# Stage 0 turned before it is decayed, four more diagonals on GpSimd, and a new order for the prologue of an RWKV-5 + MLP kernel

## The chip, the cores and the metric

The kernel runs on one core of a Trainium2 chip. A core has five engines with their own instruction streams: TensorE (PE; its weight loads are shown as PEld), VectorE (DVE), ScalarE (ACT), GpSimd (POOL) and SyncE (SP). They wait for one another by semaphores. DMAs are issued by SP, ACT and POOL. The metric is the device time of one execution in microseconds (us); lower is better. Times are medians of several executions; the profile is of one.

## The reference

Two operators, one after the other. The first is a linear attention with a decaying state, over B = 4 batches, H = 8 heads, S = 768 tokens, D = 48 channels:

```python
for t in range(S):
    kt, vt, rt = (k[:, :, t].copy(), v[:, :, t].copy(), r[:, :, t].copy())
    cur = np.einsum('bhd,bhe->bhde', u[None] * kt, vt)
    y[:, :, t] = np.einsum('bhd,bhde->bhe', rt, state + cur)
    state = w[None, :, :, None] * state + np.einsum('bhd,bhe->bhde', kt, vt)
```

The second takes y as 3072 rows of 384 and computes `h = x @ w_in` (384 to 2048), `g = maximum(0.01 * h, h)` and `g @ w_out` (2048 to 384).

## The kernel before

**Stages.** The recurrence is done in chunks of L = 128 tokens. A stage n is one chunk of one batch (chunk n // 4, batch n % 4), 24 stages in all. Within a chunk, r is multiplied by powers of w rising with the token (`qtab`) and k by falling powers (`ktab`), both centred on token 64, so that one matrix product gives the decayed scores. The letters of the list ORDER stand for these steps of a stage:

- k, r, v: loads, by DMA from POOL's queue with a cast to bf16 (stage 0's k and r come in fp32 from ACT's and SP's queues into `k_f`, `r_f`);
- P (`prep_half`, q for r and k for k): DVE multiplies by the table into the tile `qk`;
- T and t (`turn_mm`, `turn_out`): TensorE turns four pairs of heads into a PSUM bank, ACT (or DVE, with an @) copies it to `tp`; X..T (`turn_dma`) does both by a DMA transpose from SP's queue, from stage TURNED = 8 on;
- A and M (`a_mm`, `a_mask_half`): the scores, in two PSUM banks, and their masking into `at`, half a for the even heads and half b for the odd;
- the diagonal (the term with u), in two ways. For n < DIAG: X, D, Q (`diag`, `diag_mm`, `scaled_v`): DVE multiplies the turned halves, four small matmuls sum over channels, DVE scales v into `vs`, and three extra matmuls (L550) add it in `y_mm`. From DIAG on: q and Q (`row_sums`, `diag_tile`): DVE makes the token sums in three steps (L373, L375, L377), POOL writes them as diagonal matrices into both halves of `at` (L384), and M lays the masked scores over them with `copy_predicated` (L436), so that M waits for POOL too;
- Y and y (`y_mm`, `y_out`): the chunk's output, turned, in PSUM, and its copy to `xT` by ACT; K and S (`kv_mm`, `state`): the new state;
- G, J, H (`g1`, `g1_pair`, `g2`) and g, j, h: the MLP for one stage by quarters, for a pair of stages by eighths (J), and the second product; ACT does the evictions (`Prelu`), SP's queue the output DMA. F n is n fill matmuls on `ones`, whose results nobody reads.

**What sets the order.** There is no scheduler. The prologue is the list ORDER: each token adds its instructions to the streams of their engines, in that order, and `Sched` derives the semaphore waits from what is read and written. An engine does its instructions strictly in order, so an instruction that waits holds up all that stand behind it on its engine: on POOL that is compute and the issue of loads alike. PSUM has eight banks of 2 KB in a free list: `take` pops the next one when a token is listed and `give` appends it, so which mask or eviction frees the bank of a later matmul group is fixed by the list. The pair loop after it (L696 to L722) handles stages 2m and 2m + 1 in turn m, from m = FIRST // 2 = 3: eight J groups, the diagonals of the two stages `ahead` (2m + 4, 2m + 5), loads for `far` (2m + 8), P and the transposes for `later` (2m + 6), then H, A, Y, M, K, S and H. At m = 3 stages 10 and 11 are ahead, 12 and 13 later, 14 and 15 far; the list ends with the masks of 9 and 8 and the loads of 12 and 13. The first groups of J take the banks that are free, and the fifth to the eighth those that the four masks of stages 9 and 8 give back, in the order in which these are listed.

**Constants.** w is loaded as one row (`w_row`) and spread over the partitions by two fp32 matmuls of 192 columns (L295), whose logarithm times the token number gives the tables by exponentials on ACT. A copy by heads (`w_head`, `w8`), and its product with u, are turned by small matmuls (`columns_mm`) into columns for the state's decay (`wl`) and the diagonal (`wu`). The identity and the triangle are made by POOL from `ones`.

## Time and profile before

| | us |
|---|---|
| median of 3 executions (lowest, highest) | 170.09 (169.96, 170.54) |
| the profiled execution | 170.54 |
| its span in the profile | 168.8 |
| TensorE busy | 164.0 (97%) |
| DVE / ACT / POOL busy | 107.6 / 92.5 / 103.8 |
| first L619 of the pair loop (m = 3) starts | 53.52 |
| last matmul ends | 166.5 |

The busy table gives each engine's time at work, and the slices show it in tenths of 40 equal parts of the span (4.2 us each). The chain that ended last follows back from the last instruction to what released it; here it is nearly all TensorE. A timeline row gives start, length, engine, line, operation, tiles and count of instructions; in a merged row the length is that of the group. L384 is POOL's diagonal product, L222 its loads, L375 and L373 DVE's row-sum products. The profile does not show which PSUM bank a matmul takes; that follows from the list.

### The profile page before, as it was taken

The page shows a single profiled execution, that of the slowest core. Times are in us where ns is not written, and L with a number is a line of the kernel's source. Part 1 is how long each engine was busy: PE and PEld are TensorE (multiplying, and loading weights), DVE is VectorE, ACT ScalarE, POOL GpSimd, SP SyncE. Part 2 cuts the span into 40 slices and gives each one's busy share as a digit, 9 for nine tenths or more (in the row PEclk, how much of TensorE's full clock was granted, in tenths as well). Part 3 has the DMA queues.
Part 4 walks back from the last instruction along what each step waited for, and adds up shares of the span by engine and source line. Part 5 has one row for each costly group of instructions (what it writes and reads, how often), then busy time and mean ns, then how long its engine had stood idle before and what let it go on. Part 6 is the DMA issues. An engine that isn't in the chain of part 4 may idle for free.

```text
span 168.8 us, 4933 instructions
## 1 busy us (share of the span) xinstructions
PE 164.0 (97%) x2127; PEld 124.4 (74%) x2127; DVE 107.6 (64%) x215; ACT 92.5 (55%) x172; POOL 103.8 (61%) x117
## 2 busy tenths in 40 slices
PE   5999999899999999999999999999999999999994
PEld 3577899798667867867867867768768668668663
DVE  7379989884376999999859959969866050000000
ACT  3855899587123933933834835735637538449221
POOL 7999999990059979897993993993707200000000
PEclk9999999999999999999999999999999999999999
DMA  6999999999999999969999299299941011011022
GB/s 106 155 170 133 163 163 173 185 190 149 110 177 144 161 62 153 193 82 169 126 140 171 55 143 177 65 109 131 147 122 50 0 50 47 0 50 47 25 74 93
DMA packets 99146, 19.67 MB, mean 117 GB/s; under 512 B 92338, under 2 KB 99124, under 8 KB 99124
## 3 DMA queue, kind: packets, MB, share of 16 engines
q0 software_dynamic: 76512, 10.03, 93.1%
q1 hardware_dynamic: 21554, 9.12, 25.2%
q8 instruction: 17, 0.28, 0.6%
q10 hardware_dynamic: 1058, 0.20, 0.6%
q14 instruction: 5, 0.04, 0.1%
HBM read 20.45 MB, written 4.72 MB: 149 GB/s over the span
## 4 chain that ended last, share of the span: by engine, by line
PE 96%; DVE 1%; issue 1%; ACT 0%; DVEq 0%
PE ps L643 37%; PE ps L619 31%; PE ps L596 6%; PE ps L557 6%; PE ps L423 4%; PE ps L260 2%; PE ps L464 2%; PE ps L398 2%; PE ps L295 1%; PE ps L550 1%; DVE v_sb L280 1%; PE ps L451 1%; PE ps L321 0%; DVE qk L344 0%; ACT out_sb L655 0%
## 5 line engine op out<-in xcount | busy, mean ns | idle before, releaser
L643 PE MATMUL ps<-w_out_sb,gT 128*128 128x384 bf16 (+2 forms) x400 | 65.7, 320 | 0.0
L619 PE MATMUL ps<-xT,w_in_sb 128*128 128x256 bf16 x480 | 54.3, 273 | 0.0
L643 PEld LDWEIGHTS ps<-w_out_sb,gT 128*128 128x128 bf16 x400 | 37.9, 98 | 22.1
L619 PEld LDWEIGHTS ps<-xT,w_in_sb 128*128 128x128 bf16 x480 | 46.7, 98 | 6.5 <-ACT xT L571 0.2
L384 POOL TENSOR_TENSOR at<-ident,s_tok 128x512 bf16<-128x512 bf16 x32 | 35.0, 1121 | 26.8 <-DVE s_tok L377 26.8
L629 ACT ACTIVATE gT<-ps 128x512 bf16<-128x512 f32 x80 | 47.8, 597 | 6.2 <-PE ps L619 1.3
L655 ACT ACTIVATE out_sb<-ps 128x384 f32<-128x384 f32 (+2 forms) x25 | 11.9, 477 | 52.9 <-PE ps L643 52.9
L436 DVE CAST_PREDICATED at<-mask,ps 128x512 bf16<-128x512 uint16 x32 | 19.9, 684 | 15.5 <-PE ps L423 15.5
L222 POOL DMA_DIRECT2D v_sb<-in_v_dram x24 | 22.5, 953 | 0.0
L222 POOL DMA_DIRECT2D k_sb<-in_k_dram x23 | 21.6, 947 | 0.0
L222 POOL DMA_DIRECT2D r_sb<-in_r_dram x23 | 21.1, 943 | 0.0
L571 ACT ACTIVATE xT<-ps 128x384 bf16<-128x384 f32 x24 | 11.0, 492 | 6.5 <-PE ps L557 6.5
L344 DVE TENSOR_TENSOR qk<-r_sb,qtab 128x384 bf16<-128x384 bf16 x23 | 13.4, 592 | 1.9 <-DMA r_sb<-in_r_dram 1.9
L344 DVE TENSOR_TENSOR qk<-k_sb,ktab 128x384 bf16<-128x384 bf16 x23 | 13.9, 606 | 0.0
L375 DVE TENSOR_TENSOR rku<-r_sb,ku 128x384 bf16<-128x384 bf16 x16 | 12.7, 794 | 0.5
L525 DVE TENSOR_TENSOR sum_t<-ps,st 128x384 bf16<-128x384 f32 x16 | 8.8, 550 | 5.2 <-PE ps L464 5.2
L596 PE MATMUL ps<-xT,w_in_sb 128*128 128x128 bf16 x192 | 12.0, 219 | 0.0
L557 PE MATMUL ps<-at,v_sb 128*32 128x128 bf16 x384 | 11.1, 219 | 0.6 <-issue 0.6
L432 DVE TENSOR_TENSOR at<-ps,mask 128x512 bf16<-128x512 f32 x16 | 10.5, 682 | 0.9 <-PE ps L423 0.9
L606 ACT ACTIVATE gT<-ps 128x512 bf16<-128x512 f32 x16 | 9.6, 600 | 2.7 <-PE ps L596 2.1
L596 PEld LDWEIGHTS ps<-xT,w_in_sb 128*128 128x128 bf16 x192 | 10.9, 98 | 0.1
L557 PEld LDWEIGHTS ps<-at,v_sb 128*32 128x32 bf16 x384 | 8.7, 97 | 1.1 <-issue 0.7
(60 smaller groups left out, 131.7 us busy)
## 6 DMA issues: line engine op xcount, KB each, us to landing
out_dram<-out_sb SPq DMA_DIRECT2D x23, 192.0 KB, 3.9
v_sb<-in_v_dram POOLq DMA_DIRECT2D x24, 96.0 KB, 6.0
r_sb<-in_r_dram POOLq DMA_DIRECT2D x23, 96.0 KB, 5.6
k_sb<-in_k_dram POOLq DMA_DIRECT2D x23, 96.0 KB, 5.1
w_in_sb<-in_moe_w_in_dram POOLq DMA_DIRECT2D x4, 384.0 KB, 5.6
w_out_sb<-in_moe_w_out_dram POOLq DMA_DIRECT2D x4, 384.0 KB, 7.9
tp<-qk SPq DMA_TRANSPOSE x16, 4.6
k_f<-in_k_dram ACTq DMA_DIRECT2D x1, 192.0 KB, 2.8
```

Of the source, the lines that this page charges most:

```text
L222: add("pool", lambda: G.dma_start(dst, src), R=pace, W=[(which, n)], dma=f"{which}{n}")
L344: add("dve", lambda: V.tensor_tensor(qk[iq][:, H * half:H * half + H, 0:D], hd(src), hd(tab[:, :]), ALU.mult), R=[(name, n), ("qk"[half] + ...
L375: add("dve", lambda: V.tensor_tensor(rku[i2][:, :], r_of(n), ku[i2][:, :], ALU.mult), R=[("r", n), ("ku", i2)], W=[("rku", i2)])
L384: add("pool", lambda hh=hh, s_of=s_of: G.tensor_tensor(at[ia][:, hh, :, :], ident[:, :].unsqueeze(1).to_broadcast([128, NP, 128]), s_of.un ...
L436: add("dve", lambda: V.copy_predicated(at[n % NAT][:, hh, :, :], mask[:, :].bitcast(mybir.dt.uint16).unsqueeze(1).to_broadcast([128, NP, 1 ...
L557: last = PE.matmul(ps_y[32 * q:32 * q + 32, 128 * s:128 * s + 128], a, m, start=not whole and step == 0, stop=step == len(columns[q]) - 1)
L571: add("act", lambda: A.activation(xT[m % NX][:, :, 128 * half:128 * half + 128], ps_y[:, 0:HD].rearrange("p (s t) -> p s t", t=128), AF.Copy),
L596: last = PE.matmul(ps_g[:, 128 * f:128 * f + 128], w_in_sb[:, s, 128 * fb:128 * fb + 128], xT[ix][:, s, t], start=s == 0, stop=s == NSL - 1)
L619: last = PE.matmul(ps_g[:, 256 * f:256 * f + 256], w_in_sb[:, s, 128 * fb:128 * fb + 128], xT[ix][:, s, :], start=s == 0, stop=s == NSL - 1)
L629: add("act", lambda: A.activation(gT[ig][:, 2 * j:2 * j + 2, :].rearrange("p f t -> p (f t)"), ps_g[:, :], AF.Prelu, alpha=0.01), R=[key], ...
L643: last = PE.matmul(ps_o[:, 0:c1 - c0], gT[ig][:, s, 128 * half:128 * half + 128], w_out_sb[:, s, c0:c1], start=s == 0, stop=s == NFB - 1)
L655: add("act", lambda: A.activation(out_sb[io][:, c0:c1], ps_o[:, 0:c1 - c0], AF.Copy), R=[key], W=held)
```

## The change

Stage 0 (n < RAW = 1): r and k are cast to bf16 without any table (`cast`, into the new tile `raw`: k by ACT, token c0k, and r by DVE, c0q@), turned by TensorE, and decayed when they leave PSUM: DVE multiplies the bank by the new table `turned`, which holds the powers of w with channels on the partitions and tokens along the row. ACT makes it by four exponentials of the token rows `trow`, each scaled by one column of log w (token E). P of r is no longer done for stage 0; P of k is, later, for the state.

DIAG goes from 8 to 4: stages 4 to 7 get their diagonals by `row_sums` and `diag_tile`, without D, `prod`, `vs` and L550.

The constants are made differently: `w_head` is loaded twice side by side and turned in one step per half of the partitions (Cw, and Cu for its product with u); the row of w is loaded as halves in partitions 0 and 64, spread by one matmul each into adjacent banks, and has one logarithm and one exponential per table; the identity, its 8x8 corner and the triangle come from comparisons on DVE of `trow` with `tcol`; the u loads move from ACT's to SP's queue, and the order of the loads on SP is w8, r0, w, u8, u. `ones` and the fill matmuls have 128 columns instead of 256. The prologue's order is listed anew, loads included; the pair loop's code is the same.

```diff
 FIRST, NB, PACE = 6, B, 3
-TURNED, DIAG, CARRY, EXACT = 8, 8, 4, 1
+TURNED, DIAG, CARRY, EXACT, RAW, VISIT, LATE = 8, 4, 4, 1, 1, 3, 3
 ORDER = """
-w k0 r0 u8 w8 u ones tcol wi0 v0z r2 table exps one id wlz qk0 F6 bcA r1 id8 F2 bcB lnA k1 u16 wu8 ktabA F1 Cm k2 lnB U
-qtabA ktabB v0 utab P0k qtabB Wl wi3 F6 T0k P0q W C tri t0k@ F1 T0q v1 P1q t0q P2q F6 T1q X0 r3 A0 P1k t1q T2q M0a T1k
-k3 t2q D0 P2k F1 K0 t1k Q0 T2k v2 M0b t2k F1 A1 X1 v5 F2 Y0 X2 M1b A2 k4 y0 D2 M1a D1 K1 G0.0 k5 Q1 M2b G0.3 g0.0 wi1
-P3q Y1 P3k g0.3 r4 S1 T3q y1 K2 Q2 T3k t3q v3 G1.3 S2 t3k M2a G1.0 r5 g1.3 P4k Y2 X3 g1.0 r8 P5k A3 S0 y2 K5 M3b r6 T5k
-G2.3 t5k S5 k7 G2.0 g2.3 M3a G1.1 k9 g2.0 P4q G0.1 g1.1 wi2 T4k g0.1 D3 P5q K3 r7 T4q Q3 t4k T5q G2.1 S3 t5q k6 P8q Y3
-t4q P6q X5 A5 v4 g2.1 P7k A4 X4 y3 D5 T6q M4a wo3 T7k t6q G3.0 M5a v8 t7k G3.3 Q5 g3.0 wo0 M5b D4 G3.1 g3.3 P9k k8 G2.2
-M4b g3.1 P7q G1.2 wo2 g2.2 P6k T7q v6 g1.2 T6k t7q@ K4 Y5 t6k Q4 wo1 A7 y5 X6 A6 k11 S4 Y4 M7b v9 D6 y4 G3.2 M6a v10
-J2.4 M6b g3.2 J2.3 M7a v11 j2.4 J2.5 X7 j2.3 r10 D7 J2.1 j2.5 q8 r9 J2.2 j2.1 J2.6 r11 j2.2 P8k J2.0 j2.6 v7 X8T K8 Q6
-K6 j2.0 G0.2 k10 S6 Y6 g0.2 S8 J2.7 y6 H1 j2.7 P11k K9 H2 h1 S9 P10q H0 h2 P9q q9 X9T P11q K7 Q9 H3 Q7 h0 X11T S7 P10k
-X10T Q8 Y7 h3 A9 y7 A8 M9a M8a M9b M8b k12 r12 v12 k13 r13 v13
+w8 k0 r0 w u8 u wlz tcol trow qk0 r3 table tri id8 k1 ones F6 zr Cw exps v0z Wl id r1 W v0y c0k wi1 E one F13 T0k c0q@
+r2 bc wu8 Cu v0 lnw T0q C t0k u16 k3 qtab t0q F3 U ktab k2 P1q F3 A0 utab P3q X0 T1q v2 P0k M0a D0 T3q t1q v1 P1k M0b
+t3q F5 T1k wi3 P2q F2 K0 Q0 t1k wi2 T2q S0 A1 t2q v3 X1 Y0 P3k P2k D1 k5 M1b y0 T3k T2k t3k K2 M1a G0.1 k4 t2k X3 A3 Q1
+g0.1 A2 r4 D3 S2 Y1 M2b r5 K1 y1 G0.3 M2a v5 X2 G1.1 g0.3 S1 v4 D2 G1.3 M3a g1.1 M3b G0.2 wi0 g1.3 Q2 K3 r7 G1.2 g0.2
+Q3 S3 Y2 wo3 g1.2 P5k Y3 P4k y2 v9 T5k P4q y3 G2.1 q4 wo1 t5k G3.2 g2.1 wo0 G3.1 g3.2 k8 P5q T4q q5 g3.1 T4k T5q Q4
+G2.2 t4q t4k G3.3 g2.2 t5q@ G1.0 g3.3 P7q Q5 A4 g1.0 A5 G2.3 M4b G3.0 g2.3 M4a K5 k9 T7q g3.0 M5a G2.0 t7q M5b wo2 K4
+Y4 g2.0 S4 k7 Y5 y4 G0.0 S5 y5 r9 J2.4 g0.0 r8 J2.5 j2.4 J2.6 k6 j2.5 J2.3 j2.6 r6 P8k J2.7 j2.3 P9k v6 J2.2 j2.7 v8 K9
+J2.0 j2.2 S9 J2.1 v7 j2.0 H1 j2.1 q7 r11 r10 v11 P7k P8q P9q T7k X8T h1 H3 P6k Q7 P6q t7k X9T q6 k10 K6 K7 h3 T6q k11
+S6 T6k t6q K8 H2 S8 t6k v10 P11q Q6 S7 P10q A6 h2 A7 H0 M7b M6b P10k M7a X10T M6a Y7 q9 h0 Y6 y7 A8 y6 A9 P11k Q9 q8
+X11T Q8 M9b M9a M8a M8b k12 r12 v12 k13 r13 v13
 """
...
+    def twice(h):
+        return dram(h, 0, [[D, H], [0, 2], [1, D]])
+
     def tokens():
-        add("pool", lambda: G.iota(tcol[:, :], pattern=[[0, 1]], base=0, channel_multiplier=1,
+        add("pool", lambda: G.iota(tcol[:, :], pattern=[[0, 1]], base=-MID, channel_multiplier=1,
                                    allow_small_or_imprecise_dtypes=True), W=["tcol"])
+
+    def token_rows():
+        for half, (sign, base) in enumerate(((1, -MID), (-1, MID - 1))):
+            add("pool", lambda half=half, sign=sign, base=base: G.iota(
+                trow[:, half, :], pattern=[[sign, 128]], base=base, channel_multiplier=0,
+                allow_small_or_imprecise_dtypes=True), W=[("trow", half)])
...
 
         def emit():
             for _ in range(n):
-                last = PE.matmul(ps[i][:, 0:256], ones[:, 0:128], ones[:, 0:256], start=True, stop=True)
+                last = PE.matmul(ps[i][:, 0:128], ones[:, :], ones[:, :], start=True, stop=True)
             return last
 
         add("pe", emit, R=["ones"], W=[("ps", i), f"fill{n}"])
 
     def identity():
-        add("pool", lambda: G.affine_select(ident[:, :], ones[:, 0:128], pattern=[[1, 128]], compare_op=ALU.is_equal,
-                                            fill=0.0, base=0, channel_multiplier=-1), R=["ones"], W=["ident"])
+        add("dve", lambda: V.tensor_scalar(ident[:, :], trow[:, 0, :], tcol[:, 0:1], None, ALU.is_equal),
+            R=["tcol", ("trow", 0)], W=["ident"])
 
     def triangle():
-        add("pool", lambda: G.affine_select(mask[:, :], ones[:, 0:128], pattern=[[1, 128]], compare_op=ALU.is_ge,
-                                            fill=0.0, base=-1, channel_multiplier=-1), R=["ones"], W=["mask"])
+        add("dve", lambda: V.tensor_scalar(mask[:, :], trow[:, 0, :], tcol[:, 0:1], None, ALU.is_gt),
+            R=["tcol", ("trow", 0)], W=["mask"])
+
+    def small_identity():
+        add("dve", lambda: V.tensor_scalar(ident8[:, :], trow[0:H, 0, 0:H], tcol[0:H, 0:1], None, ALU.is_equal),
+            R=["tcol", ("trow", 0)], W=["ident8"])
 
...
-    half_bank = {}
-
-    def spread_w(half):
-        ps_w, key = half_bank[half] = take()
-        cols = slice(192 * half, 192 * half + 192)
-        add("pe", lambda: PE.matmul(ps_w[:, cols], one_row[:, :], w_row[:, cols], start=True, stop=True),
-            R=["one_row", "w_row"], W=[key])
-
...
+    w_bank = []
+
+    def spread_w():
+        for half in range(2):
+            w_bank.append(take())
+        assert w_bank[1][1][1] == w_bank[0][1][1] + 1
+
+        def emit():
+            for half in range(2):
+                at0 = slice(64 * half, 64 * half + 1)
+                last = PE.matmul(w_bank[half][0][:, 0:192], one_row[at0, :], w_row[at0, :], start=True, stop=True)
+            return last
+
+        add("pe", emit, R=["one_row", "w_row"], W=[w_bank[0][1], w_bank[1][1]])
...
+    def table(dst, exps, name, read):
+        add("act", lambda: A.activation(dst[:, :], lnw[:, :], AF.Exp, scale=exps[:, 0:1]),
+            R=["lnw", read], W=[name + "tab"])
+
+    def turned_table():
+        for p in range(NP):
+            add("act", lambda p=p: A.activation(turned[:, p:2 * NP:NP, :], trow[:, :, :], AF.Exp,
+                                                scale=wcol[:, p:p + 1]),
+                R=["wcol", ("trow", 0), ("trow", 1)], W=[("turned", p)])
...
+    def cast(half, eng):
+        dst, src = raw[:, H * half:H * half + H, 0:D], hd((r_of, k_of)[half](0))
+        if eng == "dve":
+            add("dve", lambda: V.tensor_copy(dst, src), R=[("rk"[half], 0)], W=[("raw", half)])
+        else:
+            add("act", lambda: A.activation(dst, src, AF.Copy), R=[("rk"[half], 0)], W=[("raw", half)])
+
     turn_bank = {}
 
     def turn_mm(n, half):
-        iq = n % NQK
+        src, reads = qk[n % NQK], [("kp" if half else "qp", n % NQK), ("qk0", n % NQK)]
+        if n < RAW:
+            src, reads = raw, [("raw", half), "raw0"]
         ps_t, key = turn_bank[n, half] = take()
...
     def turn_out(n, half, eng):
         it = n % NTP
         ps_t, key = turn_bank[n, half]
         dst = tp[it][:, NP * half:NP * half + NP, :].rearrange("p m t -> p (m t)")
-        if eng == "dve":
+        if n < RAW:
+            tab = turned[:, NP * half:NP * half + NP, :].rearrange("p m t -> p (m t)")
+            add("dve", lambda: V.tensor_tensor(dst, ps_t[:, :], tab, ALU.mult),
+                R=[key] + [("turned", p) for p in range(NP)], W=[("tp", it, half)])
+        elif eng == "dve":
             add("dve", lambda: V.tensor_copy(dst, ps_t[:, :]), R=[key], W=[("tp", it, half)])
         else:
             add("act", lambda: A.activation(dst, ps_t[:, :], AF.Copy), R=[key], W=[("tp", it, half)])
...
-    def columns_mm():
-        ps_c, key = c_bank["c"] = take()
+    def w_columns():
+        ps_c, key = c_bank["w"] = take()
 
         def emit():
             for hh in range(2):
-                rows = slice(64 * hh, 64 * hh + D)
-                PE.matmul(ps_c[rows, 0:H], w_head[:, :], ident8[:, :], start=True, stop=True)
-                last = PE.matmul(ps_c[rows, H:2 * H], wu_head[:, :], ident8[:, :], start=True, stop=True)
-            return last
-
-        add("pe", emit, R=["w_head", "wu_head", "ident8"], W=[key])
...
+                last = PE.matmul(ps_c[64 * hh:64 * hh + 64, 0:NP], w_head[:, hh, :], ident8[:, hh:H:2],
+                                 start=True, stop=True)
+            return last
+
+        add("pe", emit, R=["w_head", "w_gap", "ident8"], W=[key])
+
+    def wu_columns():
+        ps_c, key = c_bank["u"] = take()
+
+        def emit():
+            for hh in range(2):
+                last = PE.matmul(ps_c[64 * hh:64 * hh + D, 0:NP], wu_head[:, :], ident8[:, hh:H:2],
+                                 start=True, stop=True)
+            return last
+
+        add("pe", emit, R=["wu_head", "ident8"], W=[key])
...
+        ps_c, key = c_bank["w"]
+        add("act", lambda: A.activation(wcol[:, :], ps_c[:, 0:NP], AF.Ln), R=[key], W=["wcol"])
+        give(key)
...
-        "w": lambda: add("sp", lambda: SP.dma_start(w_row[:, :], row(w)), W=["w_row"], dma="w"),
-        "w8": lambda: add("sp", lambda: SP.dma_start(w_head[:, :], by_head(w)), W=["w_head"], dma="w8"),
-        "u8": lambda: add("act", lambda: A.dma_start(u_head[:, :], by_head(u)), W=["u_head"], dma="u8"),
-        "u": lambda: add("act", lambda: A.dma_start(u_row[:, :], row(u)), W=["u_row"], dma="u"),
+        "w": lambda: add("sp", lambda: SP.dma_start(
+            w_row[0:65:64, :], dram(w, 0, [[HD // 2, 2], [1, HD // 2]])),
+            W=["w_row"], dma="w"),
+        "w8": lambda: add("sp", lambda: SP.dma_start(w_head[:, :, 0:D], twice(w)), W=["w_head"], dma="w8"),
+        "u8": lambda: add("sp", lambda: SP.dma_start(u_head[:, :], by_head(u)), W=["u_head"], dma="u8"),
+        "u": lambda: add("sp", lambda: SP.dma_start(u_row[:, :], row(u)), W=["u_row"], dma="u"),
```

More of the change, by code (lines that the diff above doesn't have):

```diff
@@ L186, in bass_rwkv5_eagle__then__act_leaky_relu_kernel @@
     out_sb = [SB(f"out_sb{i}", [128, HD], FP32) for i in range(NO)]
[L187 removed]
+    ps_all = ctx.enter_context(nc.psum_tensor("ps", [128, 8, 512], FP32))
+    ps = [ps_all[:, i, :] for i in range(8)]
     V, A, PE, SP, G = nc.vector, nc.scalar, nc.tensor, nc.sync, nc.gpsimd
@@ L559, in emit @@
             return last
-        reads = [("v", n), "v0", ("at", ia, 0), ("at", ia, 1), "ident", ("tp", it, 0)]
+        reads = [("v", n), ("v0", n), ("at", ia, 0), ("at", ia, 1), "ident", ("tp", it, 0)]
         if n < DIAG:
```

78 lines of the change are left out of this document (36 added, 42 removed).

## The prediction

> **What bounds the kernel now.** I read the page's busy table and slices first, then the chain that ended last, then the timelines of DVE and POOL (GpSimd) around the place where the pair loop begins.
>
> ```profile
> PE 164.0 (97%) x2127; PEld 124.4 (74%) x2127; DVE 107.6 (64%) x215; ACT 92.5 (55%) x172; POOL 103.8 (61%) x117
> PE   5999999899999999999999999999999999999994
> DVE  7379989884376999999859959969866050000000
> POOL 7999999990059979897993993993707200000000
> ```
>
> TensorE is full in every slice but the first and last, so time is saved by giving it less work and lost wherever it has to wait. The other two rows matter as well: POOL is full up to slice 9 and DVE is full where the loop begins (slices 13 to 20).
>
> ```profile
> 12.20 0.36 DVE qk L344
> ...
> 32.73 0.27 PE ps L550 x3
> 33.00 0.51 PE ps L557 x28
> 33.51 0.18 PE ps L451 x4
> ...
> 52.25 0.17 PE ps L550 x3
> 52.42 0.50 PE ps L557 x28
> 52.92 0.55 PE ps L423 x16
> 53.47 0.05 issue
> 53.52 5.41 PE ps L619 x48
> 58.93 2.60 PE ps L643 x16
> ```
>
> These are start, length and what, from the chain in order of time. After 12.6 us it is TensorE alone. The loop begins at 53.52; a pair takes 12.33 us there (66.03 to 78.36 to 90.69). What decides whether TensorE can go on is off this chain:
>
> ```profile
> 56.54 0.55 DVE L377 TENSOR_REDUCE s_tok<-rku 128x8 f32<-128x384 bf16 x1
> 57.01 0.35 DVE L373 TENSOR_TENSOR ku<-k_sb,u_tab 128x384 bf16<-128x384 bf16 x1
> 57.39 2.97 DVE L375 TENSOR_TENSOR rku<-r_sb,ku 128x384 bf16<-128x384 bf16 x1
> 69.38 1.08 DVE L375 TENSOR_TENSOR rku<-r_sb,ku 128x384 bf16<-128x384 bf16 x1
> ```
>
> ```profile
> 48.53 4.28 POOL L384 TENSOR_TENSOR at<-ident,s_tok 128x512 bf16<-128x512 bf16 x4 [10.22 <-DVE s_tok L377]
> 52.75 0.94 POOL L222 DMA_DIRECT2D k_sb<-in_k_dram  x1
> 58.03 2.11 POOL L384 TENSOR_TENSOR at<-ident,s_tok 128x512 bf16<-128x512 bf16 x2
> 69.17 1.08 POOL L384 TENSOR_TENSOR at<-ident,s_tok 128x512 bf16<-128x512 bf16 x1 [0.65 <-DVE s_tok L377]
> ```
>
> First, a DVE product of two SBUF tiles takes 0.36 us alone but stands until the POOL diagonal product beside it is over (69.17 to 70.25 against 69.38 to 70.46; 2.97 us with two of them). Second, before the change POOL has 10.22 us of idle time and has built stages 9 and 8's diagonals by 52.8, just before the loop; then it issues stage 12's loads.
>
> The Trainium skill, SBUF — State Buffer, section Who interferes with whom, says that a VectorE instruction with two SBUF inputs and a GpSimd instruction that reads SBUF exclude each other wholly, and that who issues first wins. The 69.38 row agrees. The 57.39 row waits from before its POOL partner's shown start.
>
> **The change part by part.** The sum is made against the profiled execution, 170.54 us (span 168.8 and 1.74 around it); it is the slowest of the three, 0.45 above their median of 170.09.
>
> *Diagonals of stages 4 to 7.* TensorE loses four diag_mm (start to start 0.12, 0.10, 0.11, 0.11, as from 25.93 to 26.05) and four times the three L550 matmuls (0.26, 0.27, 0.26 and some 0.27): -1.5 us, all on the chain. DVE gives up prod and vs (0.34 + 0.46 a stage by spacing) and gets three row-sum steps (0.39 + 0.39 + 0.47), +0.45 a stage; hidden while TensorE has loads of G work listed, not hidden if POOL is at a diagonal. POOL gets eight products of 1.07, 8.6 us; its idle 10.22 us pays, so it comes to the loop with nothing to spare.
>
> *Opening.* Stage 0's transposes no longer wait for the tables, but DVE's first turned eviction waits for four exponentials of 128x256 (some 0.42 each, between the 0.35 spacing of 128x192 and 0.50 for 128x384) and stands behind the wu columns, so behind the spread of w. That is two halves of 0.97; one after the other they put the first Y at about 13.3 (13.68 before), side by side at 12.6. L423's eight matmuls from two row halves take 0.28 to 0.33, less than eight times L398's 0.055, so nearer to side by side. Either way v0 is now POOL's sixth load: issued about 6.0, with three loads' and one w_in's transfer ahead it lands near 11.7, and stage 1's masks then queue on DVE, so the second Y waits some 0.3 to 0.6. Bounds -0.7 to +0.3, taken -0.2. Fills are 32 of 128 columns instead of 26 of 256; they stand in waits, so nothing. The u loads go from ACT's queue to SP's (0.73 and 0.23 there), so ACT's table load starts a us sooner, unused since the w columns come later than that. On SP, w moves behind w8 and r0 (issue 0.80 to about 1.7), which is why the spread cannot start before about 4.4. The constants' own DVE steps (two iotas on POOL at 0.13 to 0.3, three comparisons of some 0.2) lie beside loads of k0 and r0 that land at 3.6 and 4.3. zero_raw likewise.
>
> With these two, TensorE reaches the loop near 51.8. POOL puts a floor under that: 41 loads up to stage 6's diagonal (33 at 0.875, 8 at 0.74 by spacing), eight products and about 1.0 waiting for s_tok, from 1.8 us on, ends at 46 to 47; masks of 6 and 7 (four of 0.60 and a P of 0.27), then Y6 and its eviction 1.2: 50.5 to 51.4. So I do not take more than -2.1 as the low end.
>
> *The loop's first pair.* The list now has q9 and q8 (row sums) at the very end, behind the masks of 6 and 7. Call E the loop's entry. From A7's end TensorE still has H0 2.60, two Ys of 0.51 and an eviction, 4.3 in all; DVE has 4 x 0.60 + 0.27 + 1.33 = 4.0 to s9. So s9 is ready near E-0.2, and stage 9's diagonal runs on POOL from E to E+2.1. DVE's q8 falls right under it: ku waits to 1.0, rku to 2.1 (the rows above), the sum ends at 2.9, and the first mask of 9, next in DVE's order, ends at 3.5. The fifth group of the pair takes the bank that this mask gives back, and wants it at 4 x 0.655 = 2.6: **+0.95**. Without exclusion the mask still waits for the diagonal till 2.1: +0.3. Stage 8's diagonal runs 3.05 to 5.2, its second mask to 5.95; the eighth group wants that bank at 5.5: **+0.5**. That masks slow under POOL is not seen in the trace; if they did, +0.6 more.
>
> *The second pair.* Behind those diagonals POOL issues k12 to v13 (5.5 us by the rows from 52.75 to 58.08): from E+5.2 instead of 0.8 us before the loop. r12's issue at 6.1 lands 5.0 later, at 11.1; stages 10 and 11's diagonals run 10.6 to 14.9; P of 12 and 13 are four two-input products, each put off by one of these four, and stand ahead of the first mask of 10 in DVE's order: it ends at 15.7. The second group of the second pair wants its bank at 12.33 + 1.45 + 0.65 = 14.4: **+1.35** (0 to 1.6: 0 if the Ps slip between). After that POOL has 9.9 us of work in a pair of 12.3 and catches up: nothing more (0 to 1).
>
> Sum: -1.5 - 0.2 + 0.95 + 0.5 + 1.35 = +1.1: 171.64 for an execution like the profiled one, 171.2 for the median.
>
> **Rivals.** *Faster: DVE is ahead of POOL.* If q8's products get in before stage 9's diagonal (s9 and q8 0.3 us closer, or the masks of 6 and 7 sooner), s8 is ready 1.5 earlier: 0.3 for the first pair, 0.4 for the second, -1.7 + 0.7 = -1.0: 169.1. It decides as soon as the three waits sum to under 1.7. For it: the excluded products cost nothing before, where they had slack. Against: the order leaves s9, POOL and ku within 0.2 us. *More is late: the loads.* v6, v8, v7 are now issued at 35 to 37.6, behind stage 4 and 5's diagonals, and K6, K7 want them near 43.3. The landings there were 5.3 by median but up to 12.7 us before, when a transpose by DMA was in flight; 7.5 instead of 5.3 adds about 1.5: 172.7. Against: POOL's pause lets the queue run dry first. *No change:* waits of 1.7 cancel the gain: 170.1.
>
> *A later full clock.* Eight matmuls take twice as long until about 11.5 (T in 0.43 at 8.17, 0.22 at 20.43). With the fills' columns halved the clock might come a stretch later; 2.1 us of real work stands between 11.5 and 14.9, of which waits already hide most: +0.7, 171.9. The Trainium skill, TensorE: Matmul & The Clock Gate, Part 1, has the rate released after a busy window of 3.4 us whose phase is free; by it the date would move between executions by about a window. No run here shows that.
>
> **How the numbers follow.** Forecast 0.50 (170.3 to 172.3), late loads 0.14, later clock 0.06, no change 0.11, DVE ahead 0.19. A measurement tells about 0.3% (0.5 us) from no change; so slower 0.69, same 0.12, faster 0.19. The range reaches from 169.1 (DVE ahead) to 173.0 (late loads, or clock and masks as well).
>
> **What would show it.** Right: no L451 and L550 for stages 4 to 7; the loop's first L619 at 51 to 52.5; in its first 48 an idle time of about 1 us ahead of the fifth group and some 0.4 ahead of the eighth, released by the masks on DVE; about 1.3 us ahead of the second pair's second group; DVE's L373 and its successor for stage 8 each over 1 us; stage 12's k issued some 5 us after the loop's start; from the third pair on 12.3 us again. Wrong if stage 8's products run in 0.36, if the loop starts after 53, or if idle time appears ahead of K6 or K7 with a load as its releaser.

## The result and the profile after

| | before | after |
|---|---|---|
| median, us (4 executions each) | 170.04 | 172.0 |
| the profiled execution | 170.54 | 171.95 |
| its span | 168.8 | 170.1 |
| loop's first group starts | 53.52 | 53.11 |
| second pair, third pair start | 65.86, 78.20 | 66.89, 79.51 |
| last matmul ends | 166.47 | 167.78 |

The changed kernel is slower: ratio 1.0127, 95% interval 1.0088 to 1.0167. The profiled execution of the kernel before is the slowest of its four and that of the changed kernel the fastest of its four, so the profiles differ by less (1.41 us) than the medians (1.96). The pairs' starts are those of the first L667 (L619 before) of each pair in TensorE's timeline; the chain of waits shows them some 0.2 us later. In some executions of some kernels below the granted clock was 0.98 or 0.99 and the time some 1 to 3 us longer; the ratios leave out those over 1.5% above the fastest of their kernel, so a median of all executions can lie above what its ratio says. Each ratio below is to the kernel before, run again beside it (medians of 170.15 to 170.45).

The table reads as a sum: entry -0.41, first pair 13.78 instead of 12.34 (+1.44), second pair 12.62 instead of 12.34 (+0.28), 12.33 from then on: +1.31, the +1.3 of the spans.

First the page of the changed kernel: the busy table, the slices, and the group of the loop's first product with its idle time.

```profile
PE 161.8 (95%) x2105; PEld 122.9 (72%) x2105; DVE 115.3 (68%) x224; ACT 93.6 (55%) x172; POOL 111.5 (66%) x125
PE   3999989999989799999999999999999999999994
DVE  7499999549999988999989789769966050000000
POOL 8999997999904799979899896993807200000000
...
L667 PE MATMUL ps<-xT,w_in_sb 128*128 128x256 bf16 x480 | 54.7, 273 | 1.2 <-DVE at L479 1.0
```

TensorE's busy time is 2.2 us lower (the opening's fills included), and yet the span is longer: two slices about the loop's entry (8 from 46.8, 7 from 55.3 us) are no longer full, and ahead of the loop POOL's row is near empty (0 and 4 in the slices from 46.8 and 51.0, where it was 5 and 9). DVE has 7.7 us more work. Next the end of the chain of waits, in order of time, start and length; before the change it is TensorE alone from 12.6 us.

```profile
44.87 2.09 DVE st L575
...
52.58 0.55 DVE s_tok L407
53.40 1.13 DVE ku L403
54.55 1.09 DVE rku L405
55.66 0.56 DVE s_tok L407
56.30 2.05 POOL at L414 x2
58.34 0.87 POOL k_sb L225
...
61.81 3.81 DMA r_sb<-in_r_dram
65.97 1.19 DVE qk L374
67.16 0.61 DVE at L479
67.82 4.76 PE ps L667 x42
```

From 37.2 to 56.2 us the chain is DVE's without a break: row sums and P, a product of the state (`st`) that takes 2.09 us, the masks of 7 and 6, then stage 9's row sums (52.58) and stage 8's. From there it runs over stage 8's diagonal and the loads behind it to a product P of stage 13, to stage 10's first mask, and only there back to TensorE. The timelines of POOL, DVE and TensorE at the loop's entry:

```profile
44.64 2.10 POOL L414 TENSOR_TENSOR at<-ident,s_tok 128x512 bf16<-128x512 bf16 x2
53.21 2.21 POOL L414 TENSOR_TENSOR at<-ident,s_tok 128x512 bf16<-128x512 bf16 x2 [6.47 <-DVE s_tok L407]
56.30 2.05 POOL L414 TENSOR_TENSOR at<-ident,s_tok 128x512 bf16<-128x512 bf16 x2 [0.88 <-DVE s_tok L407]
58.29 0.92 POOL L225 DMA_DIRECT2D k_sb<-in_k_dram  x1
```

```profile
39.56 3.03 DVE L374 TENSOR_TENSOR qk<-r_sb,qtab 128x384 bf16<-128x384 bf16 x2
...
44.87 2.09 DVE L575 TENSOR_TENSOR st<-sum_t,wl 128x384 bf16<-128x384 bf16 x1
...
49.14 1.28 DVE L479 CAST_PREDICATED at<-mask,ps 128x512 bf16<-128x512 uint16 x2
...
53.31 1.20 DVE L403 TENSOR_TENSOR ku<-k_sb,u_tab 128x384 bf16<-128x384 bf16 x1
54.55 1.08 DVE L405 TENSOR_TENSOR rku<-r_sb,ku 128x384 bf16<-128x384 bf16 x1
55.66 0.55 DVE L407 TENSOR_REDUCE s_tok<-rku 128x8 f32<-128x384 bf16 x1
56.13 1.93 DVE L479 CAST_PREDICATED at<-mask,ps 128x512 bf16<-128x512 uint16 x3
```

```profile
51.34 0.24 PE L605 MATMUL ps<-tp,st 128*32 128x128 bf16 x4 [0.72 <-DVE at L479]
...
53.11 2.79 PE L667 MATMUL ps<-xT,w_in_sb 128*128 128x256 bf16 x24
56.87 3.08 PE L667 MATMUL ps<-xT,w_in_sb 128*128 128x256 bf16 x24 [0.97 <-DVE at L479]
```

Stage 8's two products stand under stage 9's diagonal (1.20 and 1.08 for 0.36), and the fifth group waits 0.97 us for the mask that comes after them. But the same thing has already happened twice before the loop: a P beside stage 7's diagonal (from 39.95; the second of the two in its row takes 2.77) and the state's product beside stage 6's (from 44.64) stand 2 us and more, the masks of 7 and 6 come late (from 49.14), and Y7 waits 0.72 us. POOL meanwhile has 6.47 us without work.

### The profile page after: what moved, and what is told of

It reads as the page before. It is cut to its first block, busy times and chain, and to the rows that moved or that the text cites. A ratio compares the mean times of both kernels' runs of the same rounds, so it can differ in the third digit from the quotient of the medians.

```text
span 170.1 us, 4904 instructions
## 1 busy us (share of the span) xinstructions
PE 161.8 (95%) x2105; PEld 122.9 (72%) x2105; DVE 115.3 (68%) x224; ACT 93.6 (55%) x172; POOL 111.5 (66%) x125
## 4 chain that ended last, share of the span: by engine, by line
PE 76%; DVE 14%; POOL 3%; DMA 2%; issue 2%; ACT 1%; DVEq 0%
PE ps L691 28%; PE ps L667 27%; PE ps L644 7%; PE ps L605 5%; DVE qk L374 4%; PE ps L466 3%; PE ps L437 2%; DMA r_sb<-in_r_dram 2%; PE ps L507 2%; DVE at L479 2%; DVE st L575 2%; DVE s_tok L407 1%; DVE rku L405 1%; POOL at L414 1%; DVE sum_t L573 1%
## 5 line engine op out<-in xcount | busy, mean ns | idle before, releaser
L414 POOL TENSOR_TENSOR at<-ident,s_tok 128x512 bf16<-128x512 bf16 x40 | 43.5, 1116 | 20.8 <-DVE s_tok L407 20.8
L667 PE MATMUL ps<-xT,w_in_sb 128*128 128x256 bf16 x480 | 54.7, 273 | 1.2 <-DVE at L479 1.0
L667 PEld LDWEIGHTS ps<-xT,w_in_sb 128*128 128x128 bf16 x480 | 46.5, 98 | 8.4 <-DVE at L479 2.0
L479 DVE CAST_PREDICATED at<-mask,ps 128x512 bf16<-128x512 uint16 x40 | 25.0, 682 | 10.0 <-PE ps L466 9.6
L225 POOL DMA_DIRECT2D v_sb<-in_v_dram x24 | 21.8, 920 | 0.0
L225 POOL DMA_DIRECT2D k_sb<-in_k_dram x23 | 21.0, 919 | 0.0
L374 DVE TENSOR_TENSOR qk<-r_sb,qtab 128x384 bf16<-128x384 bf16 x23 | 14.2, 624 | 4.7 <-DMA r_sb<-in_r_dram 4.6
L405 DVE TENSOR_TENSOR rku<-r_sb,ku 128x384 bf16<-128x384 bf16 x20 | 15.4, 769 | 0.7
L619 ACT ACTIVATE xT<-ps 128x384 bf16<-128x384 f32 x24 | 11.0, 490 | 6.5 <-PE ps L605 6.2
L407 DVE TENSOR_REDUCE s_tok<-rku 128x8 f32<-128x384 bf16 x20 | 11.1, 553 | 0.7
L605 PE MATMUL ps<-tp,st 128*32 128x128 bf16 x240 | 9.4, 221 | 1.1 <-DVE at L479 0.7
```

Of the source, the lines that this page charges most:

```text
L225: add("pool", lambda: G.dma_start(dst, src), R=pace, W=[(which, n)], dma=f"{which}{n}")
L374: add("dve", lambda: V.tensor_tensor(qk[iq][:, H * half:H * half + H, 0:D], hd(src), hd(tab[:, :]), ALU.mult), R=[(name, n), "qk"[half] + ...
L405: add("dve", lambda: V.tensor_tensor(rku[i2][:, :], r_of(n), ku[i2][:, :], ALU.mult), R=[("r", n), ("ku", i2)], W=[("rku", i2)])
L407: add("dve", lambda: V.tensor_reduce(s_tok[i2][:, :], hd(rku[i2][:, :]), AX.X, ALU.add), R=[("rku", i2)], W=[("s", i2)])
L414: add("pool", lambda hh=hh, s_of=s_of: G.tensor_tensor(at[ia][:, hh, :, :], ident[:, :].unsqueeze(1).to_broadcast([128, NP, 128]), s_of.un ...
L479: add("dve", lambda: V.copy_predicated(at[n % NAT][:, hh, :, :], mask[:, :].bitcast(mybir.dt.uint16).unsqueeze(1).to_broadcast([128, NP, 1 ...
```

## The experiments

The theory: a GpSimd diagonal excludes DVE's products of two SBUF tiles (tiles that do not lie in PSUM), and the list puts such products under the diagonals of 7, 6 and 9 (under stage 8's, from 56.30, DVE has only masks); TensorE's 1.5 us are a real gain. The rivals: the mere amount of work on DVE or POOL, the late listing of 9 and 8 alone, the late loads. In all diffs below the line numbers are left out, and of a list only the part that matters is shown, wrapped anew.

**One input.** Stage 8's two products become row sums.

```diff
+    s_one, s_two = SB("s_one", [128, H], FP32), SB("s_two", [128, H], FP32)
...
         i2 = n % 4
+        if n == 8:
+            chain = ((s_one, k_of(n), ("k", n), "s1"), (s_two, r_of(n), "s1", "s2"), (s_tok[i2], k_of(n), "s2", ("s", i2)))
+            for dst, src, needs, done in chain:
+                add("dve", lambda dst=dst, src=src: V.tensor_reduce(dst[:, :], hd(src), AX.X, ALU.add),
+                    R=[needs, ("r", n), "u_tab"], W=[done])
+            return
```

> The changed kernel, but stage 8's two DVE products (ku and rku) are replaced by two more row sums, over k and over r, in the same chain of three; each reads one SBUF tile, and stage 8's diagonal is left out in this way (its numbers are meaningless). DVE has slightly more to do (0.47 for 0.39, twice). Theory (the products stand because GpSimd's diagonal of stage 9 excludes an operation with two SBUF inputs): none of the three takes over 0.6 us, s_tok of stage 8 is ready about 1.3 us sooner against the diagonal of stage 9, the first mask of 9 waits only for that diagonal; the loop's fifth group idles 0.2 to 0.4 instead of 0.97, and the time falls by 0.7 to 1.2 us: 170.8 to 171.3. Rival (the mask waits for GpSimd or for DVE's place in the list whatever the operands are): the three take longer than 0.6 under the diagonal or the mask is no sooner, 171.8 to 172.3.

171.2 us, ratio 1.0065 (1.0034 to 1.0097). DVE's timeline of this run:

```profile
53.40 0.55 DVE L407 TENSOR_REDUCE s_one<-k_sb 128x8 f32<-128x384 bf16 x1
53.98 0.55 DVE L407 TENSOR_REDUCE s_two<-r_sb 128x8 f32<-128x384 bf16 x1
54.57 0.55 DVE L407 TENSOR_REDUCE s_tok<-k_sb 128x8 f32<-128x384 bf16 x1
55.42 2.69 DVE L486 CAST_PREDICATED at<-mask,ps 128x512 bf16<-128x512 uint16 x4 [0.30 <-POOL at L421]
```

Under the same diagonal (53.30 to 57.39, now both stages without a pause) none takes longer than elsewhere. The first pair lasts 12.73 (53.20 to 65.93) instead of 13.78. The entry (53.20) and the second pair (12.62) are as they were. So about 1.05 us of the first pair's 1.44 is the exclusion of these two products: the three sums that replace them have slightly more work, and the same place in the list.

**Write only.** GpSimd's four tiles of stages 6 to 9 are written without reading.

```diff
         for hh in range(2):
+            if 6 <= n < 10:
+                add("pool", lambda hh=hh: G.memset(at[ia][:, hh, :, :], 0.0),
+                    R=["ident", ("s", n % 4)], W=[("at", ia, hh)])
+                continue
             s_of = s_tok[n % 4][:, :]...
```

> The changed kernel, but GpSimd writes the diagonals of stages 6 to 9 as plain zeros (a write that reads no tile) behind the same waits; these four stages' diagonal terms are left out. Theory (exclusion by a GpSimd operation that reads SBUF, once at stages 7 and 6 and again at 9 and 8): DVE's P and state products beside stages 7 and 6 take 0.36 instead of 2.77 and 2.09, the loop is entered 0.7 to 1.1 us sooner (52.0 to 52.4), stage 8's products take 0.36, and the first pair's waits fall from 1.4 to under 0.5: 169.8 to 170.6. If the zeros are also written faster than 1.07 us each, up to 0.5 less. Rival (the entry is set by DVE's own amount of work and by the list's order): entry at 52.8 to 53.2, 171.2 to 172.

169.32 us, ratio 0.9945 (0.9916 to 0.9974): faster than the kernel before. POOL and DVE:

```profile
40.18 1.10 POOL L414 MEMSET at<- 128x512 bf16 x2
43.71 1.12 POOL L414 MEMSET at<- 128x512 bf16 x2
52.38 0.99 POOL L414 MEMSET at<- 128x512 bf16 x2 [7.55 <-DVE s_tok L407]
```

```profile
39.87 0.62 DVE L374 TENSOR_TENSOR qk<-r_sb,qtab 128x384 bf16<-128x384 bf16 x2
44.91 0.36 DVE L579 TENSOR_TENSOR st<-sum_t,wl 128x384 bf16<-128x384 bf16 x1
48.33 1.29 DVE L483 CAST_PREDICATED at<-mask,ps 128x512 bf16<-128x512 uint16 x2 [0.81 <-PE ps L470]
52.51 0.35 DVE L403 TENSOR_TENSOR ku<-k_sb,u_tab 128x384 bf16<-128x384 bf16 x1
```

The three products that stood 1.2 to 2.8 us take 0.35 and 0.36. Entry 52.42, pairs of 12.35 and 12.33, TensorE's idle times between 12.6 and 80 us are 0.17 and a pause of 0.88 that no wait explains. A write of zeros takes 0.5 us instead of 1.07, so this run takes both the exclusion and half of POOL's time away; that DVE's products run at their own length beside the writes is the part that speaks for the exclusion. POOL's time by itself did not hold the masks of 7 and 6 in the changed kernel: stage 6's diagonal is over at 46.74 there, the first of these masks comes at 49.14, and the chain between is DVE's. Nor is it the mere amount of DVE's work: with the same instructions DVE now stands idle 2.05 us ahead of the state (44.32) and 0.81 ahead of the masks, and from 27.4 us to the loop the chain is TensorE's. The entry, 1.10 us sooner than before, is the 1.5 of removed work less the 0.17 and less 0.32 of pause (0.88 against 0.56 before): the opening by itself gave next to nothing.

**The diagonals alone.** The kernel before, with DIAG = 4 and this list (core of it):

```diff
-TURNED, DIAG, CARRY, EXACT = 8, 8, 4, 1
+TURNED, DIAG, CARRY, EXACT = 8, 4, 4, 1
-t4q P6q X5 A5 v4 g2.1 P7k A4 X4 y3 D5 T6q M4a
+t4q P6q q5 Q5 A5 v4 g2.1 P7k A4 q4 Q4 y3 T6q M4a
...
-t6k Q4 wo1 A7 y5 X6 A6 k11 S4 Y4 M7b v9 D6
+t6k wo1 q7 Q7 A7 y5 q6 Q6 A6 k11 S4 Y4 M7b v9
```

> The kernel before, with one part of the change alone: the diagonals of stages 4 to 7 by row sums and GpSimd, listed where the old way's first product stood (for stage 7 ahead of its scores). Nothing else is moved. One expectation: GpSimd's 10.2 us of idle time takes the 8.6 us of products and TensorE's 1.5 us are gained: 168.5 to 169.5. The other, which I think likelier: the products stand ahead of the loads of stages 6 to 11 on GpSimd's queue, the idle time lies behind these loads, and TensorE waits for masks and loads at stages 5 to 7: 172 to 177, the loop entered after 55.

176.63 us, ratio 1.0395 (1.0329 to 1.0460); loop entry 61.50. TensorE's waits, in total, times, longest:

```profile
PE ps L596 <- DVE at L436: 3.0, 1, 3.0
PE ps L619 <- DVE sum_t L525: 1.9, 1, 1.9
```

The profiled execution took 178.53 us, the longest of the four. The second expectation held: the 10.2 us of idle time lie behind the loads, and the diagonals now stand ahead of them. Both waits have the exclusion in them as well: ku and rku take 1.20 and 1.08 us (from 26.66) beside stage 5's diagonal, with stage 4's diagonal and the mask of the first wait behind them, and a rku of 2.37 (from 37.31) beside stage 7's stands ahead of the sum of the second. In this order the diagonals lose more than they save.

**The opening alone.** The changed kernel with DIAG = 8: q4 to q7 and Q4 to Q7 become X, D and Q of the old way in the new list.

```diff
-TURNED, DIAG, CARRY, EXACT, RAW, VISIT, LATE = 8, 4, 4, 1, 1, 3, 3
+TURNED, DIAG, CARRY, EXACT, RAW, VISIT, LATE = 8, 8, 4, 1, 1, 3, 3
-P11q Q6 S7 P10q A6 h2 A7 H0 M7b M6b P10k M7a X10T M6a Y7 q9
+P11q S7 P10q X6 A6 D6 h2 X7 A7 D7 H0 M7b M6b P10k M7a Q7 X10T M6a Q6 Y7 q9
```

> The changed kernel with its other part alone: stage 0, the constants and the new order stay, the diagonals of stages 4 to 7 are made in the old way (prod, four small matmuls, scaled v, three matmuls more) in the new order. TensorE has its 1.5 us again. Theory (the late listing of stages 9 and 8's row sums makes the first pair wait, whatever stages 4 to 7 do; the opening by itself gives nothing): the loop is entered at 53.2 to 53.9, the fifth group still waits 0.6 to 1.1 us, 171.2 to 172.3. Rival (the diagonals of 4 to 7 on GpSimd make the loss): entry near 53 and no wait in the first pair, 169.3 to 170.1.

173.35 us, ratio 1.0170 (1.0133 to 1.0206): longer than either expectation, and above the whole change, though the two intervals meet. Entry 53.63 (53.11 with the four diagonals); the first pair lasts 13.54 and the second 13.63. The theory's waits are there without any diagonal of stages 4 to 7: the list's late q9 and q8 suffice. What was not expected is the second pair:

```profile
66.75 0.59 DVE L374 TENSOR_TENSOR qk<-r_sb,qtab 128x384 bf16<-128x384 bf16 x1 [1.53 <-DMA r_sb<-in_r_dram]
67.26 1.19 DVE L374 TENSOR_TENSOR qk<-k_sb,ktab 128x384 bf16<-128x384 bf16 x1
68.37 2.47 DVE L479 CAST_PREDICATED at<-mask,ps 128x512 bf16<-128x512 uint16 x4
```

Stage 13's r was issued at 62.09 and landed at 66.7, 1.1 us later than in the changed kernel, and the first mask of stage 10 stands behind its P: 1.3 us lost in the second pair, where the changed kernel loses 0.28.

**The loads ahead.**

```diff
-P11q Q6 S7 ... P11k Q9 q8 X11T Q8 M9b M9a M8a M8b k12 r12 v12 k13 r13 v13
+P11q Q6 k12 r12 v12 k13 r13 v13 S7 ... P11k Q9 q8 X11T Q8 M9b M9a M8a M8b
```

> The changed kernel; only the six loads of stages 12 and 13 are listed behind stage 6's diagonal instead of at the end, so that GpSimd issues them in its 6.47 us of idle time ahead of stage 9's diagonal. Theory (the chain of waits of the changed kernel goes through both diagonals, these loads, r of stage 13 and its product P to the second pair's second group): that group's wait of 0.3 us is gone, since P of 12 and 13 comes before the diagonals of 10 and 11; the first pair's waits stay at 0.97 and 0.3; 171.4 to 171.9, and the third pair begins at 79.2 to 79.5 instead of 79.68. Rival (the second pair's wait is the row sums' and diagonals' own lateness, not the loads'): the group waits as before, 171.8 to 172.2.

171.92 us, ratio 1.0115 (1.0085 to 1.0145). The second pair's wait is gone (67.11 to 79.44, 12.33) and the first pair's is as before (13.77), as the theory had it; the third pair begins at 79.44 in the timeline, 79.61 in the chain, by which it was expected at 79.2 to 79.5 instead of 79.68. The entry was 0.23 later, at 53.34, and the time can't be told from the changed kernel's.

**Stage 9's sums ahead.**

```diff
-h3 T6q k11 S6 ... Q6 k12 r12 v12 k13 r13 v13 S7 P10q ... Y7 q9 h0 Y6 y7 A8 y6 A9 P11k Q9 q8 X11T Q8
+h3 T6q q9 k11 S6 ... Q6 k12 r12 v12 k13 r13 v13 S7 Q9 P10q ... Y7 q8 h0 Y6 y7 A8 y6 A9 P11k X11T Q8
```

> As the run with the loads ahead, and the row sums of stage 9 also go ahead of the state of stage 6 (its diagonal behind the six loads), those of stage 8 ahead of Y6. Nothing is left out or added: only DVE's and GpSimd's order changes. Theory (the first pair waits because stage 9's and 8's sums come last in DVE's order, so that a product of 8 falls under the diagonal of 9): stage 9's diagonal is over and stage 8's begun by the loop's entry, the fifth and eighth groups wait 0 to 0.2 us. DVE has stage 9's three steps (1.3 us) ahead of the masks of 7 and 6, and a product may now stand under stage 6's diagonal, so the entry is 53.1 to 53.9; 170.3 to 171.2. Rival (the waits come with the amount of GpSimd's and DVE's work, and only move): the entry is 1.3 to 2 us later instead, 171.6 to 172.6.

175.56 us, ratio 1.0332 (1.0298 to 1.0367). Half of the expectation held: no wait is left in the loop (56.88, 69.22, 81.56: 12.34 each). The other half fell, and so did my price for it: the entry is at 56.88, not 53.9.

```profile
44.91 2.28 DVE L405 TENSOR_TENSOR rku<-r_sb,ku 128x384 bf16<-128x384 bf16 x1
...
49.89 1.19 DVE L374 TENSOR_TENSOR qk<-r_sb,qtab 128x384 bf16<-128x384 bf16 x1
...
53.32 1.13 DVE L374 TENSOR_TENSOR qk<-k_sb,ktab 128x384 bf16<-128x384 bf16 x1
```

Stage 9's product now falls under stage 6's diagonal, another P under stage 9's (from 52.13; the P from 49.89 stands beside loads alone), and the masks of 7 and 6 stand behind both: TensorE waits 3.17 us for them at 55.11 (0.72 in the changed kernel), and 0.78 and 0.47 for states ahead of that. The wait was moved, as the rival had it, and grew beyond the rival's price too.

**Relisted as a whole, three ways.** The code of the changed kernel, the list from stage 3 on in another order (its core; the rows of 4 and 5 move as well).

```diff
-P7k P8q P9q T7k X8T h1 H3 P6k Q7 P6q t7k X9T q6 k10 K6 K7 h3 T6q k11
-S6 T6k t6q K8 H2 S8 t6k v10 P11q Q6 S7 P10q A6 h2 A7 H0 M7b M6b P10k M7a X10T M6a Y7 q9 h0 Y6 y7 A8 y6 A9 P11k Q9 q8
+A7 T6k P6q r11 X8T t6k X9T Q7 M7b Q6 K6 T6q h3 H2 M7a S6 t6q P10q A6 h2 k11 K8 H0 P10k q9 M6b r12 Y7 h0 M6a Y6 Q9 S8
+v11 y7 A9 k12 y6 K7 q8 X10T M9b Q8 v13 A8 v10 M9a r13 P11q M8a P11k S7 v12 k13 M8b X11T
```

> The changed kernel with its code as it is and the list from stage 3 on laid out anew, by hand of the rows: row sums and diagonals of 7, 6 and 9 sooner, the P of stages 8 to 11 where GpSimd issues loads instead of under diagonals, the masks of 7 and 6 ahead of most P, stage 12 and 13's loads spread between the diagonals, K6 and K7 behind. Theory (TensorE's 1.5 us less work is a real gain that the exclusion and the late row sums took back twice): entry at 51.6 to 52.4, no wait over 0.3 us in the first two pairs, 168.4 to 169.3, faster than the kernel before by 0.5% to 1%. Rival (the work on DVE and GpSimd is too much for the stretch from 35 to 60 us in any order): 170 or more.

170.77 us, ratio 1.0044 (1.0011 to 1.0077). In the profiled execution the entry is at 52.76, but stage 10's transpose by DMA, now issued late, holds the first pair:

```profile
PE ps L466 <- DMA tp<-qk: 1.6, 1, 1.6
```

That execution took 173.29 us, 2.5 above the median; how long the others wait there is not shown.

Two more lists put the transposes sooner; the core of the first of them:

```diff
+... q7 P9q j2.0 P7k H1 T7k t7k t7q X9T j2.1 P8q h1 X8T H3 P6k A7 v6 v8 r10 q6 K6 P6q h3 T6k T6q r11 Q7 H2 t6k M7a t6q M7b
+Q6 S6 P10q q9 A6 M6a P10k k11 h2 K8 H0 M6b Y7 k12 X10T Q9 S8 P11q h0 Y6 v12 P11k y7 y6 A9 q8 r12 v11 Q8 M9b M9a ...
```

> The changed kernel's code once more, the list from stage 3 on in another order: as in the first relisting, but the transposes of stages 11 and 10 are no longer issued at the very end (they took 5 to 7 us there and stage 10's scores waited 1.6 us for them), and no mask stands behind more than one product that can fall under a diagonal. Theory (the loss is the order, the gain TensorE's 1.5 us): entry at 52.0 to 52.6, no wait over 0.3 us after it, 168.7 to 169.6. Rival (DVE, GpSimd and the DMA queue have too little slack from 35 to 60 us, whatever the order: one wait goes, another comes): 170.0 to 172.

> A third order of the same code, with the row sums of 7 and 6 directly behind each other, K7 ahead of K6 and more of the loads ahead of stage 6's diagonal. Theory: as for the second relisting, 168.7 to 169.6, with the entry at 52.0 to 52.8 and no wait over 0.3 us after it. Rival: a wait for a load or a mask of stage 6 or 7 of over 1 us, 170 to 172.5.

171.66 us, ratio 1.0072 (1.0037 to 1.0107), and 171.74 us, ratio 1.0081 (1.0056 to 1.0106). Both have pairs of 12.33 from the entry on (54.25 and 54.65, later than expected) and one large wait ahead of it, both times for a P: 1.85 us at 42.84 in the first, 1.75 at 27.68 in the second. The second's is a P of 3.03 us that began at 24.50, with a diagonal from 25.10; the first's is this, the second row beside stage 7's diagonal (from 40.33):

```profile
38.84 1.19 DVE L374 TENSOR_TENSOR qk<-r_sb,qtab 128x384 bf16<-128x384 bf16 x1 [0.15 <-DMA r_sb<-in_r_dram]
39.95 2.75 DVE L374 TENSOR_TENSOR qk<-k_sb,ktab 128x384 bf16<-128x384 bf16 x1
```

**Stage 7's diagonal later, then its P first.** Two single steps from the first of these lists: k of 11 and 12 ahead of Q7, and on top of it P7k ahead of q7.

```diff
-K6 P6q h3 T6k T6q r11 Q7 H2
+K6 P6q h3 T6k T6q r11 k11 k12 Q7 H2
```

> The second relisting with two loads (k of stages 11 and 12) moved ahead of stage 7's diagonal on GpSimd's queue, nothing else. In that relisting the only wait of TensorE over 0.4 us is 1.85 us at 42.84 for stage 7's P of k, which stood 2.75 us under that diagonal (P from 39.95, diagonal from 40.33); GpSimd then idles 2.09 us ahead of stage 6's diagonal. Theory (one excluded product is the whole loss): with the diagonal starting near 42.1, P takes 0.35, the wait at 42.84 is gone, entry at 52.3 to 52.7, the third pair at 77.2 to 77.6, and the time 169.2 to 170.0 by the relisting's median, under the kernel before's by 0.2 to 1.0 us. Rival (some other product comes under the diagonal, or the state of stage 6 or the masks of 7 wait for it): a wait of over 1 us elsewhere, 170.5 to 172.

```diff
-J2.1 q7 P9q j2.0 P7k H1 T7k
+J2.1 P7k q7 P9q j2.0 H1 T7k
```

> The run with stage 7's diagonal later, with one more token moved: stage 7's P of k goes ahead of stage 7's row sums and stage 9's P of r on DVE, so that it runs as soon as k of stage 7 has landed (near 38.1). In the run before, that P waited for its turn and then stood 1.19 us, and TensorE waited 1.15 us for it at 42.04, its only wait. Theory (that one wait is what keeps this order from the kernel before's time less 1.1): no wait over 0.4 us, entry at 52.2 to 52.6, 169.2 to 170.0. Rival (DVE is the bound in this stretch, and the 1.15 us come back at the transposes of stage 6 or the masks of 7): a wait of 0.7 us or more there, 170.4 to 171.2.

170.79 us, ratio 1.0038 (1.0014 to 1.0061), then 172.1 us over all executions with a ratio of 1.0023 (0.9990 to 1.0056). The profiled execution of the second is 170.20, its span 168.4, entry 53.10, third pair at 77.77 (78.20 before). In the first run P9 and P7 took 1.23 and 1.19 us although the diagonal began only at 42.16 and POOL issued loads beside them, so the wait was 1.15 instead of 1.85; in the second it went to the transpose of stage 6 (0.69 at 45.34), whose P stood 2.67 us from 42.61, as the rival had it. DVE has no gap of over 0.2 us from 38.1 to 47.2 in the first. In all five relistings the median missed the theory's range.

**Half of it.** Stages 4 and 5 from GpSimd, 6 and 7 the old way, the list laid out for that (not shown; the second edit stands wherever DIAG told the two ways apart).

```diff
+OLD = (0, 1, 2, 3, 6, 7)
-        if n < DIAG:
+        if n in OLD:
```

> The changed opening, but only stages 4 and 5 get their diagonals from GpSimd; 6 and 7 have the old way (prod, four small matmuls, scaled v, three matmuls more), and the list from stage 4 on is laid out for that: row sums and diagonals of 9 and 8 go into the time in which the changed kernel builds 7's and 6's. TensorE saves 0.75 us of the 1.5. Theory (the collisions come from four diagonals more than GpSimd has idle time for beside DVE's products): no wait over 0.4 us in the loop's first two pairs, entry at 52.6 to 53.3, 169.3 to 170.2. Rival (any relisting of this density meets a late load or a product under a diagonal): a wait of over 1 us, 170.5 to 172.5.

173.1 us, ratio 1.0122 (1.0081 to 1.0163): entry 55.50, clean pairs after it, and 2.4 us of waits for `prod` of 6 and 7. One of these took 1.26 us (from 49.26) beside stage 8's diagonal, and a rku ahead of it 2.26 (from 42.56) beside stage 9's: the old way's `prod` has two SBUF inputs as well. The rival's wait came, and the median is above its range too.

## Why the prediction was right, and where it was not

Forecast 171.2 (range 169.1 to 173.0), measured 172.0, slower as forecast. The forecast change was +1.1; the profiled executions differ by 1.41, the medians by 1.96. The parts below are compared in the profiles (spans +1.3). That the total came out near is luck: the loop is entered 1.29 us later than forecast, and the second pair loses 1.07 less.

- *Removed work, -1.5:* right. TensorE is busy 40.3 us between 12.6 and the loop before, 38.8 after; of the fourteen runs the one with writes alone turned most of it into time.
- *Opening, -0.2:* within its bounds, but nothing of it reached the loop. The first Y came 0.7 us sooner (12.99 for 13.68), between the forecast's two cases (12.6 and 13.3), although the halves of w's spread ran side by side (1.01 for four matmuls against 1.00 for two); yet what TensorE has left to do at 12.6 is less by the diagonals' 1.5 alone. TensorE's full clock comes at some 12.2 instead of 11.5 (four turns take 0.61 from 11.36 and 0.40 from 12.32; before, four take 0.63 from 10.31 and eight 0.64 from 11.42); that rival was not tried by itself.
- *Loop entered at 51.8 (-1.7):* the step that failed. It was 53.11. The floor that POOL puts under it was right in its parts: stage 6's diagonal ended at 46.74 (46 to 47 was said), the masks of 7 and 6 with their P take 2.74 from 49.14 (2.67), and 1.23 more lead to the loop (1.2). What it put at nothing are the 2.4 us between. DVE is then still behind with states and P, because a P stood 2.77 us beside stage 7's diagonal and the state's product 2.09 beside stage 6's. I priced the exclusion only where the list ended, at stages 9 and 8, and let DVE reach the masks of 7 and 6 with nothing in its way; the row that said otherwise was quoted (2.97 us for one product). For TensorE it is a wait of 0.72. Pauses of 0.51 and 0.38 instead of 0.56 make 0.33 more; such pauses, which no wait explains, come to 0 to 0.9 us in the fourteen traces, and one input, with 0.43 of them, enters no sooner (53.20). Write only, where the exclusion is gone, enters at 52.42. By the prediction's own test ("wrong if the loop starts after 53") this step is wrong.
- *First pair, +0.95 and +0.5:* right in sum and cause: +1.44, with ku and rku of stage 8 at 1.20 and 1.08. From one matmul's start to the next it is 0.11 us in these groups elsewhere (48 in 5.24), 1.24 ahead of the fifth and 0.39 ahead of the eighth: 1.13 and 0.28 lost. The mask that frees the eighth's bank ended 5.96 after the entry (5.95 was said), so what the fifth loses more the eighth loses less. One input shows that without exclusion 0.39 is left (0.3 was said).
- *Second pair, +1.35:* right mechanism, size off: 0.28. Stage 12's r landed 3.7 us after its issue, not 5.0, so stage 12's first P started at 62.90, ahead of the diagonals (63.56), and stage 13's alone held the mask. It hangs on one landing: with r of 13 1.1 us later, the opening alone lost 1.3 here. The loads ahead took it to nothing.
- *Later pairs, 0; masks under POOL:* right. Pairs of 12.33; the masks' mean is 682 ns, the same in write only.
- *The rivals:* DVE ahead of POOL did not occur; the waits summed to 1.7 in the loop and 0.72 ahead of it. No wait of TensorE for v6, v8 or v7 appears ahead of K6 and K7.
- *A reading:* before the change TensorE was not full in every slice but the first and last; the eighth is an 8, and holds the pause of 0.56.

That the order alone could win the 1.5 us back was my next theory, and it is not shown: of the five relistings four took the loop's waits to zero, and each of the five had one of 0.7 to 1.85 us somewhere from 27 to 63 us. None beats the kernel before; the nearest is level with it. Whether some order does is open. What write only shows is narrower: with diagonals that read no SBUF, and are written twice as fast, this same list is 0.5% faster.

## What to carry to other kernels

When work moves to an engine with idle time, ask which products on other engines it will exclude, stage by stage from the first to the last, not only where the waits are already visible. Idle time behind a queue of loads is not idle time for work listed ahead of them. Where two engines are full over the same stretch, moving one product early moves the wait; price what stands behind it before taking the gain.
